# A fused convolution and expert-routing kernel: the second part's convolution moved into the first part's routing, one-hot matrices made apart, and a token load issued later

## The chip, the cores and the metric

The kernel runs on one core of one Trainium2 chip. The metric is the device time of the whole program in microseconds, the median of three executions. The profile is one further execution, taken by the hardware profiler; its span is 45 us shorter than the timed runs, so only differences are carried from one to the other.

## What is computed

The input `x` has 8 sequences of 3584 tokens of 192 channels. A causal convolution with 7 taps comes first: the taps are a softmax of `weight` over the 7 places, one set for each of 8 heads of 24 channels. Then each token goes through one of 8 experts:

```
logits     = y @ w_gate                      # 8 values a token
local_gate = sigmoid(y @ w_local)
e = argmax(logits)  if first of its sequence or local_gate < 0.5
    else the expert of the token before it
out = softmax(logits)[e] * relu(y @ w1[e]) @ w2[e]      # 192 -> 1024 -> 192
```

The expert of a token can depend on that of the token before, so routing is a scan along the sequence. Everything is in float32.

## The kernel before

**Parts and blocks.** The 28672 tokens are cut into 16 parts of 1792. Each part is convolved, its logits are taken, it is routed, and its rows (weight, token number, 192 channels) are scattered to a table in DRAM, `slots`, that has a region for each expert. In the text a *put* is one such scatter: `indirect_dma_start` of GpSimd, the line with `slots<-y_sb,posi`. A *block* is one unit of 128 rows of one expert (from block 35 on, mostly two units). For a block the kernel loads its rows back (`xg<-slots`, `load_rows`) and its expert's weights (`wb<-in_w`, `load_w`, 1.5 MB), transposes the rows on TensorE (`turn`), multiplies by the first matrix (`hidden`, hps), applies relu on ScalarE (hT), multiplies by the second (`output`, yps), adds the two halves on ScalarE (L961) and VectorE (L965) into `o_sb`, and scatters that to the output (`out_dram<-o_sb,xg`, L969). There are two buffers of `o_sb`, so the ScalarE step of block i waits until the output scatter of block i-2 has landed. Part 0 gives at least 7 full units, so blocks 0 to 6 need part 0 alone, and block 7 is the first that needs part 1 to be routed and all its puts landed.

**The first two parts** are done by another way than the later ones, because TensorE has nothing else to do: `wide` convolves by matmul (16 products with a banded matrix `hank`, 8 for each half of the part), turns the result (`turned`, 6 groups of transposes), takes the logits (`products`) and turns those back (`lps`, `lsb`, `ltp`, `lt`). `wide_route` then routes the part: VectorE finds the maximum and the local gate (`fc`), TensorE transposes it (`rps`), VectorE scans twice (`run`), TensorE transposes back (`bps`) and adds up the one-hot counts (`tot`, `within`), and VectorE makes the positions (`pos`, `posi`) and, for part 0, `first_table`, the list of the first seven units. Each of these is a Python generator that stops at its `yield`s; the calls of `next` decide how the two are woven together. All PSUM tiles called hps share four buffers, so a matmul into a fifth one waits for the eviction of an earlier one, and a tile that is still to be read (`rps`) takes one of the four out of the rotation meanwhile. In part 1 all evictions are ScalarE's.

**The first two blocks** are not read back from `slots`, because that would take too long. Their rows are picked from `ya` by one-hot matrices on TensorE: VectorE makes `hot` in 2 x 4 instructions (L526), and `gather` multiplies (L533, 16 products for each of the two blocks).

**Later parts** are convolved by multiply-add on VectorE (`conv`, L384, 48 instructions a part, the first tap by ScalarE, L374) and routed by `route`. Both are generators again, and `step(time)` runs about so many microseconds of them between the stages of a block. `x_in[g]` is the part's token load, 1920 KB (L115).

**Order of work.** The engines run the program's order: the kernel uses a manual schedule. All plain loads are in one queue, SyncE's, which the profile calls q1: weights, rows and tokens are issued in the program's order, and an issue that waits holds up those behind it. Indirect scatters are GpSimd's (q0). `load_w(j)` of block j is issued at block j-3, when the buffer of block j-4 is free; `load_rows` of block j waits for the puts of its part.

Of the kernel before, what the change touches and what calls it, by code (L numbers as in the profile page):

```python
# [8 lines left out]
F32 = mybir.dt.float32  # L9
I32 = mybir.dt.int32  # L10
Act = mybir.ActivationFunctionType
Alu = mybir.AluOpType
# [65 lines left out]
def kernel(  # L78
# [55 lines left out]
    with tc.tile_pool(name="scr", bufs=1) as scr:  # L134
        w = scr.tile([1, H, KC], F32, name="w")
        nc.scalar.dma_start(out=w, in_=weight.rearrange("(o h) k -> o h k", o=1))

        nc.sync.dma_start(out=hank, in_=wh)
        x_in = {0: load_b(0)}
        wg = cst.tile([P, 3 + DQ, Q], F32, name="wg")  # L140
        nc.scalar.dma_start(out=wg, in_=wgl)
        x_in[1] = load_b(1)
        nc.gpsimd.memset(ones, 1.0)
        any_ = scr.tile([1, 1], F32, name="any_")
        nc.scalar.activation(any_, ones[:1, :1], Act.Exp)
        make_identity(nc, ident)

        def awake(n):

            ps = hps_p.tile([P, 512], F32, name="hps")  # L150
            for _ in range(n):
                nc.tensor.matmul(ps[:, :P], lhsT=ones, rhs=ones, start=True, stop=True)

        awake(3)

        wide_w = scr.tile([P, 2 * H + H * KC], F32, name="wide_w")
        nc.vector.memset(wide_w, 0.0)
        wm = wide_w[:1, :H]
        nc.vector.tensor_reduce(wm, w, axis=AX.X, op=Alu.max)
        nc.vector.tensor_scalar(wm, wm, -1.0, None, Alu.mult)  # L160
        cps = hps_p.tile([P, 512], F32, name="hps")
        nc.tensor.matmul(cps[:, :H], lhsT=ones, rhs=wide_w[:, :H], start=True, stop=True)
        nc.vector.tensor_copy(nm, cps[:, :H])
        awake(7)
        ws = wide_w[:1, H:]
        wc = ws[:, H:].rearrange("o (h k) -> o h k", k=KC)
        nc.vector.tensor_tensor(w, w, bcast(wm, KC), op=Alu.add)
        nc.scalar.activation(w, w, Act.Exp)
        for h in range(H):
# [16 lines left out]
    def z_tile():  # L186
        return yt.tile([P, 3 * NH * TB + NB * DR], F32, name="z")

    def wide(g, xv, y_sb, zy, both):

        yT = zy[:, :3 * NH * TB].rearrange("p (u s) -> p u s", s=TB)
        yr = zy[:TB, 3 * NH * TB:].rearrange("p (b d) -> p b d", d=DR)
        lps = yps_p.tile([P, 512], F32, name="yps")[:, :4 * TB].rearrange("p (q s) -> p q s", s=TB)
# [64 lines left out]
        if both:  # L261
            nc.vector.tensor_copy(lsb[:, :2, :], lps[:, :2, :])
            nc.scalar.copy(lsb[:, 2:, :], lps[:, 2:, :])
        else:
            nc.scalar.copy(lsb, lps)
        ltp = yps_p.tile([P, 512], F32, name="yps")[:TB].rearrange("p (q c) -> p q c", c=P)
        for q in range(4):
            nc.tensor.transpose(ltp[:, q, :], lsb[:, q, :], identity=ident)
# [94 lines left out]
    def conv(g, x_sb):  # L363
        y_sb = row_tile()[:, :NT, :]
        got[g] = y_sb

        def cols(h):
            return y_sb[:, :, Y0 + h * GS:Y0 + (h + 1) * GS]

        def chans(h, k):  # L370
            return x_sb[:, k:k + NT, h * GS:(h + 1) * GS]

        def first(h):
            nc.scalar.activation(cols(h), chans(h, 0), Act.Copy, scale=c[:, h, 0:1])  # L374

        first(0)
        yield 0
        for h in range(H):
            if h + 1 < H:
                first(h + 1)  # L380
            if h == H // 2 and g + 1 < NPART:
                x_in[g + 1] = load_x(g + 1)
            for k in range(1, KC):
                nc.vector.scalar_tensor_tensor(cols(h), chans(h, k), c[:, h, k:k + 1],  # L384
                                               cols(h), Alu.mult, Alu.add)
                yield 0.6
# [3 lines left out]
    def wide_route(g, y_sb, lt):  # L390
# [29 lines left out]
        for a in range(2):  # L420
            nc.tensor.transpose(rps[:, a, :], fc[:, a, :], identity=tr)
        rs = sm.tile([P, NB], F32, name="rs")[:TB]
        nc.vector.tensor_reduce(rs, ex, axis=AX.X, op=Alu.add)
        nc.vector.tensor_scalar(rs, rs, 1e-9, None, Alu.add)
        nc.vector.reciprocal(rs, rs)
        yield
        run = sm.tile([NB, TB], F32, name="run")
        nf = sm.tile([NB, TB], F32, name="nf")
# [18 lines left out]
        tot = nps[:, :E * (1 + NB)].rearrange("p (e b) -> p e b", b=1 + NB)  # L447
        within = nps[:TB, E * (1 + NB):E * (1 + 2 * NB)]
        nc.tensor.matmul(tot[:, :, 0], lhsT=ones[:1, :], rhs=place[0:1, :], start=True, stop=True)
        yield  # L450
        oh = sm.tile([P, E, NB], F32, name="oh", bufs=1)[:TB]
        nc.vector.tensor_tensor(oh, bcast_mid(bps, E), bcast(en[:TB], NB), op=Alu.is_equal)
# [24 lines left out]
        yield  # L477
        if g == 0:
            first_table(upto[:, :, NB], pos)
        nc.vector.tensor_copy(place, upto[:, :, NB])  # L480
        nc.vector.tensor_tensor(base, place, eo, op=Alu.subtract)
        if g:
# [3 lines left out]
    def first_table(upto, pos):  # L486
# [33 lines left out]
        rel = sm.tile([P, 2, NB], F32, name="rel", bufs=1)[:TB]  # L520
        nc.vector.scalar_tensor_tensor(rel, bcast(r2[:TB], NB), -float(UT), bcast_mid(pos, 2),
                                       Alu.mult, Alu.add)
        for i in range(2):
            for b in range(0, NB, NB // 4):
                bs = slice(b, b + NB // 4)
                nc.vector.tensor_tensor(hot[:TB, i, bs, :], bcast(rel[:, i, bs], UT),  # L526
                                        bcast_mid(slot[:TB], NB // 4), op=Alu.is_equal)
        nc.vector.tensor_tensor(used, end[:, 1:], end[:, :E], op=Alu.subtract)

    def gather(i, y_sb, ps, blocks):  # L530

        for b in blocks:
            nc.tensor.matmul(ps[:, :Y0 + D], lhsT=hot[:TB, i, b, :], rhs=y_sb[:TB, b, :Y0 + D],  # L533
                             start=(b == 0), stop=(b == NB - 1))
# [440 lines left out]


    LEAD = 2
    st = {"conv": 1, "cgen": None, "route": 1, "rgen": None, "routed": 1}

    def start_conv():  # L980
        g = st["conv"] + 1

        free = not any(p[0] <= g - 3 for p in to_put)
        if st["cgen"] is None and g < NPART and g <= st["route"] + LEAD and free:
            st["conv"] = g
            st["cgen"] = conv(g, x_in.pop(g))
            next(st["cgen"])
# [20 lines left out]
    def step(time):  # L1008
# [17 lines left out]
    ya, yb = row_tile(), row_tile()  # L1026
    hot = row_tile().rearrange("p a b -> p (a b)")[:, :2 * NB * UT].rearrange(
        "p (i b s) -> p i b s", i=2, b=NB)
    for _ in wide(0, x_in.pop(0), ya, z_tile(), True):
        pass  # L1030
    x_in[2] = load_x(2)
    wide1 = wide(1, x_in.pop(1), yb, z_tile(), False)
    for i, _ in enumerate(wide_route(0, ya, got.pop(0))):
        for _ in range([4, 6, 0, 0, 0][i]):
            next(wide1)
    while to_put:
        put()
    for _ in wide1:
        pass

    wbs, xgs = {}, {}

# [21 lines left out]
    weights(AHEAD - 1)  # L1064


    picks = [yps_p.tile([P, 512], F32, name="yps") for _ in range(2)]
    more = wide_route(1, yb, got.pop(1))
    next(more)
    gather(0, ya, picks[0], range(NB // 2))  # L1070
    next(more)
    gather(0, ya, picks[0], range(NB // 2, NB))
    xgs[0] = gathered(picks[0])
    gather(1, ya, picks[1], range(NB // 2))
    next(more)
    step(2.4)
    xT, _ = turn(blocks[0][1], xgs[0])
    gather(1, ya, picks[1], range(NB // 2, NB))
    next(more)
    step(2.4)  # L1080
    xgs[1] = gathered(picks[1])
    for _ in more:
        pass
    for _ in range(6):
        put()
    for i, (_, n, _, _) in enumerate(blocks):
        ensure(i)
        weights(i + AHEAD)
        hT = hidden(n, wbs[i], xT)
        if i + 1 < len(blocks):  # L1090
            xT, copied = turn(blocks[i + 1][1], xgs[i + 1])
            if len(to_put) > NT // 2 and n == KT:
                put(copied)
        step(2.1 if n == 1 else 4.2)
        output(n, wbs.pop(i), xgs.pop(i), hT)
        step(1.3 if n == 1 else 3.0)
# [80 lines left out]
```

## Time and profile before

| | before |
|---|---|
| median of three executions | 1378.92 us (1378.63 to 1378.95) |
| span of the profiled execution | 1333.7 us |
| TensorE busy | 1315.8 us, 99% of the span |
| VectorE busy | 780.4 us, 59% |
| ScalarE busy | 512.1 us, 38% |
| GpSimd busy | 490.9 us, 37% |
| mean DMA rate | 255 GB/s |
| granted TensorE clock | 1.00 of full speed |

TensorE is nearly always busy, so what can change the time is where it waits. Its waits stand in the first 93 us: the convolution and routing of the first two parts until 49.7 us, and the first blocks after it. From there on a block of one unit follows the last every 5.5 us. A start time in an answer of the trace is counted from the start of the span; "x48" means 48 records of one kind, and what stands in brackets is the idle time of the engine before it and what ended that.

### The profile page before, as it was taken

How to read it: one execution, taken by the hardware profiler on the slowest of the kernel's cores; microseconds unless marked ns; L12 is line 12 of the kernel's file. 1: busy time of each engine (PE TensorE's matmuls, PEld its weight loads, DVE VectorE, ACT ScalarE, POOL GpSimd, SP SyncE). 2: the span in 40 equal slices, each digit the busy share in tenths (PEclk: the TensorE clock that was granted, in tenths of full speed). 3: DMA queues.
4: the chain of work that ended last, by engine and by line, in shares of the span. 5: the costliest groups of instructions: out<-in, count | busy, mean ns of one | idle time of the engine just before them, and what ended most of it. 6: DMA issues, size and time to landing. Idle time of an engine off the chain costs nothing. (4 is left out here: it accounts for less than half of the span.)

```text
span 1333.7 us, 41873 instructions
## 1 busy us (share of the span) xinstructions
PE 1315.8 (99%) x17140; PEld 1250.9 (94%) x17140; DVE 780.4 (59%) x2414; ACT 512.1 (38%) x1151; POOL 490.9 (37%) x534
## 2 busy tenths in 40 slices
PE   8989999999999999999999999999999999999998
PEld 7889999999999999999999999999999999999997
DVE  5989898877878787878787878786500000000000
ACT  5344444433333333333333333333333333333333
POOL 3734354434434343444343434343443211111111
PEclk9999999999999999999999999999999999999999
DMA  5899999976767576767676767565665555556893
GB/s 184 318 349 417 383 389 366 381 263 238 283 210 275 209 275 210 271 214 274 211 274 211 273 213 273 211 216 210 216 224 209 189 192 192 197 187 234 319 321 126
DMA packets 67299, 340.39 MB, mean 255 GB/s; under 512 B 12576, under 2 KB 23191, under 8 KB 47650
## 3 DMA queue, kind: packets, MB, share of 16 engines
q1 hardware_dynamic: 44640, 284.73, 58.9%
q0 software_dynamic: 22320, 52.82, 10.5%
q8 instruction: 136, 2.23, 0.7%
q14 instruction: 57, 0.47, 0.1%
q10 hardware_dynamic: 146, 0.15, 0.0%
HBM read 284.73 MB, written 53.41 MB: 254 GB/s over the span
## 5 line engine op out<-in xcount | busy, mean ns | idle before, releaser
L953 PE MATMUL yps<-wb,hT 64*128 64x192 f32 x7328 | 630.9, 325 | 3.9 <-ACT hT L942 3.4
L937 PE MATMUL hps<-xT,wb 64*128 64x256 f32 (+1 forms) x6816 | 627.0, 336 | 1.9 <-issue 1.9
L937 PEld LDWEIGHTS hps<-xT,wb 64*128 64x128 f32 x6816 | 560.3, 187 | 45.6 <-issue 2.9
L953 PEld LDWEIGHTS yps<-wb,hT 64*128 64x128 f32 x7328 | 597.1, 187 | 4.7 <-ACT hT L942 3.6
L969 POOL DMA_INDIRECT out_dram<-o_sb,xg x229 | 231.5, 1011 | 627.1 <-DVE o_sb L965 557.4
L384 DVE SCALAR_TENSOR_TENSOR y_sb<-x_sb,c,y_sb 128x336 f32<-128x336 f32 x672 | 383.6, 583 | 47.1 <-ACT y_sb L374 29.6
L942 ACT ACTIVATE hT<-hps 128x512 f32<-128x512 f32 (+1 forms) x568 | 261.1, 512 | 359.9 <-PE hps L937 359.8
L965 DVE SCALAR_TENSOR_TENSOR o_sb<-yps,xg,o_sb 128x192 f32<-128x192 f32 x229 | 87.4, 413 | 443.3 <-ACT o_sb L961 427.7
L754 POOL DMA_INDIRECT slots<-y_sb,posi x228 | 229.5, 1007 | 190.1 <-ACT hT L942 110.7
L961 ACT ACTIVATE o_sb<-yps,xg 128x192 f32<-128x192 f32 x229 | 86.8, 417 | 413.4 <-PE yps L953 404.5
L923 ACT COPY xT<-xps 128x768 f32<-128x768 f32 (+1 forms) x142 | 97.0, 683 | 1.9 <-PE xps L356 1.9
L356 PEld LDWEIGHTS xps<-ident,xg 64*128 64x128 f32 x1374 | 68.2, 139 | 8.4 <-DMA xg<-slots 0.3
L356 PE MATMUL xps<-ident,xg 64*128 64x64 f32 x1374 | 69.6, 222 | 0.1
L374 ACT ACTIVATE y_sb<-x_sb,c 128x336 f32<-128x336 f32 x112 | 63.6, 591 | 0.0
L549 DVE STREAM_TRANSPOSE z<-y_sb 128x768 f32<-128x768 f32 (+1 forms) x56 | 44.3, 846 | 0.1
L575 DVE COPY lt<-lq 32x36 f32<-32x36 f32 x224 | 41.7, 186 | 3.3
L559 PE MATMUL hps<-z,wg 64*32 64x128 f32 x1344 | 24.1, 273 | 0.4 <-issue 0.4
L559 PEld LDWEIGHTS hps<-z,wg 64*32 64x32 f32 x1344 | 19.5, 105 | 4.6 <-issue 3.1
L567 DVE STREAM_TRANSPOSE lq<-ls 128x256 f32<-128x256 f32 x14 | 6.2, 445 | 13.3 <-ACT ls L564 13.3
L545 POOL COPY y_sb<-y_sb 128x896 f32<-128x896 f32 x14 | 13.3, 948 | 0.1
L651 DVE COPY bk<-so_far 1x32 f32<-1x32 f32 x56 | 12.3, 219 | 0.7
L207 PE MATMUL hps<-x_sb,wb 118*112 118x192 f32 x64 | 11.7, 330 | 0.8 <-DMA x_sb<-in_xb_dram 0.8
(240 smaller groups left out, 370.8 us busy)
## 6 DMA issues: line engine op xcount, KB each, us to landing
wb<-in_w_dram SPq DMA_DIRECT2D x138, 1536.0 KB
x_sb<-in_x_dram SPq DMA_DIRECT2D x14, 1920.0 KB
xg<-slots SPq DMA_DIRECT2D x87, 259.0 KB
xg<-slots SPq DMA_DIRECT2D x53, 129.5 KB
wb<-in_w_dram SPq DMA_DIRECT2D x12, 512.0 KB
out_dram<-o_sb,xg POOLq DMA_INDIRECT x229
slots<-y_sb,posi POOLq DMA_INDIRECT x228
x_sb<-in_xb_dram SPq DMA_DIRECT2D x4, 768.0 KB
```

The costliest lines, as they stand in the source:

```text
L356: nc.tensor.transpose(to, src[rows], identity=ident[rows, rows])
L374: nc.scalar.activation(cols(h), chans(h, 0), Act.Copy, scale=c[:, h, 0:1])
L384: nc.vector.scalar_tensor_tensor(cols(h), chans(h, k), c[:, h, k:k + 1], cols(h), Alu.mult, Alu.add)
L549: nc.vector.transpose(z[:, t:u, :], y_sb[:, t:u, Y0:Y0 + D])
L754: ins = nc.gpsimd.indirect_dma_start(out=slots[:, :], in_=rows, in_offset=None, out_offset=bass.IndirectOffsetOnAxis(ap=to, axis=0)).ins
L923: copied = nc.scalar.copy(to, at)
L937: nc.tensor.matmul(hps[half][:, j, w], lhsT=wb[rows, f0:f0 + P], rhs=xT[rows, d, w], start=(d == 0 and j == 0), stop=(d == KD - 1), skip_g ...
L942: relu = nc.scalar.activation(hT[:, m:m + 2, w], hps[half][:, :, w], Act.Relu)
L953: nc.tensor.matmul(yps[half][:, k * D:(k + 1) * D], lhsT=hT[rows, m, k * P:(k + 1) * P], rhs=wb[rows, WA + m * D:WA + (m + 1) * D], start= ...
L961: nc.scalar.activation(o_sb[:, k, :], y[k][0], Act.Copy, scale=xg[:, k, 0:1])
L965: nc.vector.scalar_tensor_tensor(o_sb[:, k, :], y[k][1], xg[:, k, 0:1], o_sb[:, k, :], Alu.mult, Alu.add)
L969: sent = nc.gpsimd.indirect_dma_start(out=out, in_=o_sb[:, k, :], in_offset=None, out_offset=bass.IndirectOffsetOnAxis(ap=xg.bitcast(I32)[ ...
```

## The change

Four things are changed.

1. `wide` of part 1 starts earlier: two of its convolution products go between the logits of part 0 and the transposes that turn these back, and 7, 6 and 1 further steps go into the first three stages of part 0's routing, where 4 and 6 stood before. The 7 are products; the 6 are four products and the first two groups of transposes; the 1 is a product. The remaining steps follow part 0's routing. `wide` takes its own z tile.
2. The one-hot matrices are made by a function `hots(i)`: that of block 0 still in part 0's `first_table`, that of block 1 only after the first stage of part 1's routing. In part 1's routing the reciprocal of the softmax sum (`norm`) comes after the scans, not before. The gathers are cut at 4 and at 9 blocks of tokens, and the first four products of block 0's gather stand ahead of the transposes of part 1's logits.
3. The tokens of the fourth part, `x_in[3]`, are loaded at the start of block 3 and no longer in the middle of part 2's convolution; part 3's convolution may not start before block 6.
4. The gate weights `wg` are loaded on SyncE's queue, between the token loads of parts 0 and 1, and no longer on ScalarE's.

```diff
-        nc.scalar.dma_start(out=wg, in_=wgl)
+        nc.sync.dma_start(out=wg, in_=wgl)
...
-            if h == H // 2 and g + 1 < NPART:
+            if h == H // 2 and 2 < g < NPART - 1:
                 x_in[g + 1] = load_x(g + 1)
...
+        if g == 0:
+            norm()
         yield
...
         nc.tensor.matmul(tot[:, :, 0], lhsT=ones[:1, :], rhs=place[0:1, :], start=True, stop=True)
+        if g:
+            norm()
...
         if g == 0:
             first_table(upto[:, :, NB], pos)
+            hots(0)
...
+    LATE = 3
...
-        if st["cgen"] is None and g < NPART and g <= st["route"] + LEAD and free:
+        if (st["cgen"] is None and g < NPART and g <= st["route"] + LEAD and free
+                and (g != 3 or g in x_in and st["block"] > LATE + 2)):
...
-    for _ in wide(0, x_in.pop(0), ya, z_tile(), True):
-        pass
+    some(wide0, WIDE)
+    some(wide1, 2)
+    rest(wide0)
     x_in[2] = load_x(2)
-    wide1 = wide(1, x_in.pop(1), yb, z_tile(), False)
-    for i, _ in enumerate(wide_route(0, ya, got.pop(0))):
-        for _ in range([4, 6, 0, 0, 0][i]):
-            next(wide1)
+    route0 = wide_route(0, ya, got.pop(0))
+    for n in (7, 6, 1, 0, 0):
+        next(route0)
+        some(wide1, n)
...
-    next(more)
-    gather(0, ya, picks[0], range(NB // 2))
-    next(more)
-    gather(0, ya, picks[0], range(NB // 2, NB))
+    gather(0, ya, picks[0], range(4))
+    rest(wide1)
+    route1 = wide_route(1, yb, got.pop(1))
+    next(route1)
+    hots(1)
+    gather(0, ya, picks[0], range(4, NB))
+    next(route1)
     xgs[0] = gathered(picks[0])
-    gather(1, ya, picks[1], range(NB // 2))
-    next(more)
-    step(2.4)
+    picks.append(yps_p.tile([P, 512], F32, name="yps"))
+    gather(1, ya, picks[1], range(9))
+    next(route1)
+    step(1.8)
...
+        if i == LATE:
+            x_in[3] = load_x(3)
```

More of the change, by code (lines that the diff above doesn't have):

```diff
@@ L187, in z_tile, with wide @@
         return yt.tile([P, 3 * NH * TB + NB * DR], F32, name="z")
-    def wide(g, xv, y_sb, zy, both):
+    WIDE = 25
+    def wide(g, xv, y_sb, both):
+        zy = z_tile()
         yT = zy[:, :3 * NH * TB].rearrange("p (u s) -> p u s", s=TB)
@@ L265, in wide @@
             nc.scalar.copy(lsb, lps)
+        yield
         ltp = yps_p.tile([P, 512], F32, name="yps")[:TB].rearrange("p (q c) -> p q c", c=P)
@@ L422, in wide_route, with norm @@
         rs = sm.tile([P, NB], F32, name="rs")[:TB]
-        nc.vector.tensor_reduce(rs, ex, axis=AX.X, op=Alu.add)
-        nc.vector.tensor_scalar(rs, rs, 1e-9, None, Alu.add)
-        nc.vector.reciprocal(rs, rs)
+        def norm():
+            nc.vector.tensor_reduce(rs, ex, axis=AX.X, op=Alu.add)
+            nc.vector.tensor_scalar(rs, rs, 1e-9, None, Alu.add)
+            nc.vector.reciprocal(rs, rs)
+        if g == 0:
+            norm()
         yield
@@ L522, in first_table, with hots @@
                                        Alu.mult, Alu.add)
[L523 to L527, printed above, removed]
-        nc.vector.tensor_tensor(used, end[:, 1:], end[:, :E], op=Alu.subtract)
+        rels.append(rel)
+        nc.vector.tensor_tensor(used, end[:, 1:], end[:, :E], op=Alu.subtract)
+    rels = []
+    def hots(i):
+        for b in range(0, NB, NB // 4):
+            bs = slice(b, b + NB // 4)
+            nc.vector.tensor_tensor(hot[:TB, i, bs, :], bcast(rels[0][:, i, bs], UT),
+                                    bcast_mid(slot[:TB], NB // 4), op=Alu.is_equal)
     def gather(i, y_sb, ps, blocks):
@@ L977 @@
     LEAD = 2
-    st = {"conv": 1, "cgen": None, "route": 1, "rgen": None, "routed": 1}
+    LATE = 3
+    st = {"block": 0, "conv": 1, "cgen": None, "route": 1, "rgen": None, "routed": 1}
     def start_conv():
@@ L1028, with some, rest @@
         "p (i b s) -> p i b s", i=2, b=NB)
-    for _ in wide(0, x_in.pop(0), ya, z_tile(), True):
-        pass
+    wide0 = wide(0, x_in.pop(0), ya, True)
+    wide1 = wide(1, x_in.pop(1), yb, False)
+    def some(work, n):
+        for _ in range(n):
+            next(work)
+    def rest(work):
+        for _ in work:
+            pass
+    some(wide0, WIDE)
+    some(wide1, 2)
+    rest(wide0)
     x_in[2] = load_x(2)
-    wide1 = wide(1, x_in.pop(1), yb, z_tile(), False)
-    for i, _ in enumerate(wide_route(0, ya, got.pop(0))):
-        for _ in range([4, 6, 0, 0, 0][i]):
-            next(wide1)
+    route0 = wide_route(0, ya, got.pop(0))
+    for n in (7, 6, 1, 0, 0):
+        next(route0)
+        some(wide1, n)
     while to_put:
         put()
-    for _ in wide1:
-        pass
+    rest(route0)
+    some(wide1, WIDE - 16)
     wbs, xgs = {}, {}
@@ L1064 @@
     weights(AHEAD - 1)
-    picks = [yps_p.tile([P, 512], F32, name="yps") for _ in range(2)]
-    more = wide_route(1, yb, got.pop(1))
-    next(more)
-    gather(0, ya, picks[0], range(NB // 2))
-    next(more)
-    gather(0, ya, picks[0], range(NB // 2, NB))
+    picks = [yps_p.tile([P, 512], F32, name="yps")]
+    gather(0, ya, picks[0], range(4))
[5 more added lines that the diff above has]
+    next(route1)
     xgs[0] = gathered(picks[0])
-    gather(1, ya, picks[1], range(NB // 2))
-    next(more)
-    step(2.4)
+    picks.append(yps_p.tile([P, 512], F32, name="yps"))
+    gather(1, ya, picks[1], range(9))
+    next(route1)
+    step(1.8)
     xT, _ = turn(blocks[0][1], xgs[0])
-    gather(1, ya, picks[1], range(NB // 2, NB))
-    next(more)
+    gather(1, ya, picks[1], range(9, NB))
+    next(route1)
     step(2.4)
     xgs[1] = gathered(picks[1])
-    for _ in more:
-        pass
+    rest(route1)
     for _ in range(6):
@@ L1086 @@
     for i, (_, n, _, _) in enumerate(blocks):
+        st["block"] = i
         ensure(i)
         weights(i + AHEAD)
+        if i == LATE:
+            x_in[3] = load_x(3)
         hT = hidden(n, wbs[i], xT)
```

## The prediction

> **What bounds the kernel now.** I read the page's first part, then TensorE's waits, its timeline where they stand, and the queue behind each wait. TensorE is busy 1315.8 of 1333.7 us, so the change can only earn back single waits. After block 0 they are three. From the waits and TensorE's timeline:
>
> ```profile
> ACT o_sb L961 <- DMA out_dram<-o_sb,xg: 7.1, 1, 7.1
> PE yps L953 <- ACT hT L942: 3.4, 1, 3.4
> PEld xps L356 <- DMA xg<-slots: 0.3, 1, 0.3
> ...
> 23.15 0.35 PE L421 MATMUL hps<-ident,fc 112*16 112x112 f32 x2 [0.84 <-ACT y_sb L214]
> 40.19 0.36 PE L421 MATMUL hps<-ident,fc 112*16 112x112 f32 x2 [0.97 <-DVE fc L415]
> 49.73 2.95 PE L937 MATMUL hps<-xT,wb 64*128 64x128 f32 x48
> 59.20 2.70 PE L953 MATMUL yps<-wb,hT 64*128 64x192 f32 x29 [0.45 <-DVE o_sb L965]
> 73.91 2.87 PE L953 MATMUL yps<-wb,hT 64*128 64x192 f32 x32 [3.42 <-ACT hT L942]
> 92.35 0.40 PE L356 MATMUL xps<-ident,xg 64*128 64x64 f32 x6
> ```
>
> The first matmul of block 0 stands at 49.73. Block 1's output waits 0.45 us for VectorE's half of block 0's output. Block 3's output waits 3.42 us for ScalarE, which itself sat 7.1 us in L961 of block 2 because the output scatter of block 0 had not landed. The last line, the transposes of block 7's rows, waits 0.3 us for the rows: small, but it is the point at which part 1's puts and SyncE's queue meet TensorE. SyncE's queue and GpSimd's, and the busy time by stretch:
>
> ```profile
> 29.92 1.17 POOL L754 DMA_INDIRECT slots<-y_sb,posi  x1 [7.16 <-issue]
> 62.63 1.01 POOL L969 DMA_INDIRECT out_dram<-o_sb,xg  x1 [0.30 <-DVE y_sb L384]
> ...
> 53.33 1.49 SPq L890 DMA_DIRECT2D xg<-slots  x2
> 58.24 0.33 SPq L883 DMA_DIRECT2D wb<-in_w_dram  x1
> 58.63 0.45 SPq L115 DMA_DIRECT2D x_sb<-in_x_dram  x1
> 72.66 0.33 SPq L890 DMA_DIRECT2D xg<-slots  x1
> 73.56 3.62 SPq L883 DMA_DIRECT2D wb<-in_w_dram  x2
> 90.27 1.25 SPq L890 DMA_DIRECT2D xg<-slots  x2
> ...
> 50.00:58.00 8.00, 8.00 (x134) 8.00 (x134) 7.24 (x32) 3.24 (x9) 4.55 (x6) 1.00 0.54 137
> 58.00:74.00 16.00, 12.13 (x184) 11.70 (x180) 12.13 (x24) 5.39 (x15) 9.99 (x11) 1.00 1.03 409
> 74.00:92.00 18.00, 18.00 (x348) 17.58 (x348) 16.65 (x38) 8.21 (x24) 8.66 (x9) 1.00 0.84 327
> ```
>
> Sixteen puts of part 0 follow 29.92 at 1.245 us each (last at 49.24); then the rows of blocks 2 and 3 (53.33), then weights. From 58 us the 16 DMA engines are full (share 1.03, 409 GB/s) until about 88 us; the mean over 58 to 88 is 402 GB/s. The scatter issued at 62.63 lands only before 72.7. The rows of block 7 are issued at 90.27.
>
> **What the Trainium skill says.** "DMA: Bandwidth & Descriptors", section "Queues, rings and completion order": each DMA engine takes turns between the queues packet by packet, and within a ring consumes in order. The trace agrees: a scatter beside large weight and token packets took 9 us from the end of its issue. The same page, "Issuing engines are not separate DMA queues": all run on the same 16 engines, so moving `wg` to another queue adds no bandwidth; that load is not in any wait here. "Perfetto Trace Analysis", "Optimization Strategy": look for the gaps on the engine to be optimised and for the semaphore behind each; that gave the three above.
>
> **The change, part by part.**
>
> *Convolution of part 1 inside part 0's routing.* Nothing is added or removed; TensorE's order changes. Before, `rps` (L421) needed one ScalarE eviction and went at 23.15. Now nine convolution products precede it, and with four hps buffers it needs the sixth eviction. ScalarE is idle from 20.5 to 22.44 and can do two there; then the exponential (22.44, waits for VectorE) stands ahead of the rest, at 0.31 us each: the sixth ends at 24.0. `rps` goes at 24.1: +1.0. Between `rps` and `bps` now stand four products and eight transposes (8 x 0.10 us); the third product needs the eviction behind ScalarE's two copies L220 and L221 (0.52 us apart), and the transposes wait for the second scan because it frees the buffer of `rps`. That gives `bps` at 27.7 against 25.84 and the end of the totals at 29.1 against 27.1. So part 0's positions, its table and its puts come 2.0 us later: first put 31.9, last 51.2, rows of block 2 issued at about 55.3, and weights behind them equally late. What could hide it: nothing on GpSimd, whose puts are back to back.
>
> *One-hot matrices apart, `norm` later, gathers cut anew.* VectorE's work is the same. The four instructions of `hots(1)` (2.5 us, half of the 5.02 of L526) move behind part 1's `fc`. VectorE makes `hots(0)` from 34.6 to 37.1, `fc` by 39.75, `hots(1)` by 42.2, the second scan by 44.3. TensorE: first gathers 35.3 to 36.6, logits turned by 37.0, 12 gather products (24 records at 0.165) to 41.0, so the 0.97 wait before L421 is gone; nine more to 44.2, `bps` 44.4, transposes of block 0 to 45.1, seven more to 47.4, counts 47.6 (VectorE, after 0.7 for `norm` and four L384 at 0.58), block 0 at about 48.2: 1.5 us early.
>
> But VectorE does not follow. Its chain to the end of block 0's L965 holds the same instructions, starts 2.0 later and recovers the 1.4 us it sat idle at 42.84 waiting for ScalarE: L965 ends between 1 us earlier and 0.7 us later than 59.14, I take +0.3. Block 1's output would be ready at 58.2 - 1.5 and waits for that. So the 1.5 us are back in that wait, and TensorE runs on from about 59.5.
>
> *Tokens of part 3 in block 3.* Before, 1920 KB stood in the ring behind block 4's weights and ahead of block 5's rows and weights, and the scatter of block 0, issued at 62.63, shared the engines with them. Now block 5's rows (small) and weights stand there. The scatter is issued at 63.3, after the same eight puts, but more of these run beside the 512 KB chunks of block 3's weights, and the rows follow sooner. I expect it landed by 67 to 70.5, against 72.6; it is wanted at 66. So block 3's output starts at 70.8 to 71.7 instead of 73.91; the 3.42 us go wholly or largely. With them gone, block 7's transposes could start at 92.05 - 3.4 + 0.3 = 88.9.
>
> The load is not removed, however: it is now behind block 6's weights and ahead of block 7's, and block 7's rows stand behind all of them. The same bytes, 10.2 MB on SyncE's queue and about 2.1 MB of scatters at 402 GB/s, 31 us, lie ahead of these rows as before, and the stream begins 2.0 us later. Before, block 7's weights were moved by 87.3 with stragglers to 89, and then the queue was empty until part 1's last put had landed and the rows went at 90.27. Now the puts land earlier (about 86) and the rows are already queued: 89 + 2.0, less 0.3 for one put more done before the stream starts, plus 0.4 for 129.5 KB: about 91.0. TensorE waits there 2 us, and block 7 starts 1.3 us earlier than at 92.35. What is behind that wait: the whole rest of TensorE's order.
>
> *Part 3's convolution from block 6.* VectorE idles some 6 us about 85 to 91. It is at 59% and has nothing to do in the last quarter of the span; part 3 is needed from block 35. Its first ScalarE instruction waits for the tokens, which land about 86, before it is reached at 90. Cost nothing. `wg` lands some us later, is needed at 14.78: nothing.
>
> **The rivals.**
>
> 1. *Likeliest: the wait moves to block 7's rows.* For it: DMA share 1.03 in the stretch, the ring's order. Gain 1.3 us: 1377.6.
> 2. *Faster: the rows come in time.* The queue was empty from 89 to 90.3, so bandwidth was not the last limit before, and the rate may be above 402 when small packets are spread otherwise. Then the gain is that of the removed wait, 92.35 - 88.9 = 3.4: 1375.5. Against it: block 7's weights and 1920 KB stand ahead.
> 3. *Slower: the 2.0 us of part 0's routing show.* Every put, row and weight of the first blocks hangs on them; if the stream also keeps its stragglers and the engines lose some throughput to the turns, block 7 starts at 94.4 to 96, or a ScalarE wait for tokens or for scatters of blocks 1 to 4 comes back beside the late token load: +2 to +3.7, about 1382.0. Against it: before, 4 us passed between the end of the stream and block 7, and half of these are now used.
>
> **How the numbers follow.** I give 0.50, 0.31 and 0.19. The bound of 0.2% is 2.76 us. Case 1 gives 0.04 faster, 0.45 same and 0.01 slower; case 2 0.27 faster and 0.04 same; case 3 0.03 same and 0.16 slower. The forecast is 1377.6. The range takes in case 2 to its middle (1375.2) and case 3 up to +2.1 (1381.0); the unknown is one scatter's landing (67 to 70.5) and the stream's end (plus or minus 1.5 us).
>
> **What would show it.** First put at 31.9 and `rps` at 24.1; block 0 at 48.2; a longer wait of block 1's output for L965 (0.45 to about 3 us); no wait, or under 1 us, at block 3's output; rows of block 7 issued about 87 with a wait of about 2 us at their transposes, at 91. Wrong if block 7's transposes start below 89.5 (rival 2) or above 94 (rival 3), or if a new wait appears after 93 us.

## The result, and the profile after

| | us, median | range | ratio to before, 95% interval |
|---|---|---|---|
| before | 1378.78 (6 runs) | 1376.51 to 1379.57 | |
| after | 1368.10 (6 runs) | 1365.55 to 1369.86 | 0.9923 (0.9910 to 0.9936) |

The change makes the kernel 0.8% faster. The forecast was 1377.6 (1375.2 to 1381.0): the time lies below the range.

The profiled execution of before took 1335.45 us, its timed ones 1379. The profiled execution of after took 1369.86, as its timed ones did. So the two pages are not a pair, and what lies between them had to be found first. TensorE's waits after, with the total, the number and the longest in us:

```profile
PE hps L453 <- DVE run L451: 6.3, 1, 6.3
PE yps L969 <- ACT hT L958: 4.5, 16, 0.3
PE hps L953 <- issue: 4.1, 8, 0.9
```

None of the three waits of before is there. In their place stand one long wait for VectorE ahead of block 0, sixteen short ones for the relu, and stops in which TensorE waits for nothing that the profile shows ("issue"). The timeline after, for TensorE, VectorE and GpSimd:

```profile
41.21 0.36 PE L425 MATMUL hps<-ident,fc 112*16 112x112 f32 x2 [1.57 <-DVE ex L412]
...
48.10 1.05 PE L549 MATMUL yps<-y_sb 112*128 112x194 f32 x3 [0.39 <-issue]
55.41 0.27 PE L453 MATMUL hps<-ident,run 16*112 16x16 f32 x1 [6.26 <-DVE run L451]
...
62.22 3.15 PE L953 MATMUL hps<-xT,wb 64*128 64x128 f32 x48
...
70.64 0.51 PE L953 MATMUL hps<-xT,wb 64*128 64x128 f32 x4 [0.45 <-issue]
72.10 0.47 PE L953 MATMUL hps<-xT,wb 64*128 64x128 f32 x3 [0.95 <-issue]
...
53.19 0.26 DVE L438 COPY nf<-hps 16x112 f32<-16x112 f32 x1 [9.62 <-remote]
...
49.70 0.94 POOL L770 DMA_INDIRECT slots<-y_sb,posi  x1 [0.30 <-issue]
64.90 0.94 POOL L770 DMA_INDIRECT slots<-y_sb,posi  x1 [14.26 <-ACT hT L958]
```

TensorE's transposes in L425 are over at 41.6. VectorE's copy of them (L438) starts at 53.19: the signal (the semaphore change that lets VectorE go on) is 11 us late, and VectorE sits idle for 9.62 of them. GpSimd issues part 0's sixteen puts back to back from 30.06 on, the last from 49.70 to 50.64. In block 1 (68 to 76) TensorE gets through one to four products each 0.7 to 1.5 us, while GpSimd issues part 1's first puts back to back from 64.90 to 74.8. The granted clock falls in these stretches (the length and TensorE's busy time stand behind the window, the granted clock third from the end):

```profile
0.00:42.00 42.00, 36.98 (x240) 29.80 (x241) 23.10 (x87) 20.94 (x52) 18.11 (x65) 1.00 0.60 214
42.00:80.00 38.00, 25.96 (x190) 23.10 (x192) 20.42 (x65) 6.77 (x21) 16.63 (x17) 0.69 0.55 190
80.00:110.00 30.00, 29.03 (x498) 27.24 (x497) 21.83 (x42) 11.69 (x33) 13.24 (x13) 1.00 0.86 316
```

The Trainium skill, "TensorE: Matmul & The Clock Gate", Part 1, says that TensorE's clock is halved after an idle window of about 3.4 us and released after a busy one. The trace agrees in the length: the stretches at half clock last 3.4, 6.8 and 13.7 us. It does not agree that the window has to be idle: in the 3.41 us ahead of each of the three TensorE was busy for 1.50, 1.78 and 1.42 us. The first begins at 42.2, behind the wait of 1.57 us; in block 1 the stop begins at 68 and the half clock at 72.9. So the half clock follows the stops and does not start them.

### The profile page after: what moved, and what is told of

Same layout as the page of the kernel before. It is cut to its first block, busy times and chain, and to the rows that moved or that the text cites. A ratio compares the mean times of both kernels' runs of the same rounds, so it can differ in the third digit from the quotient of the medians.

```text
span 1368.2 us, 41873 instructions
## 1 busy us (share of the span) xinstructions
PE 1335.7 (98%) x17140; PEld 1299.4 (95%) x17140; DVE 776.1 (57%) x2414; ACT 513.8 (38%) x1151; POOL 490.8 (36%) x534
## 3 DMA queue, kind: packets, MB, share of 16 engines
q0 software_dynamic: 22320, 52.82, 10.2%
## 5 line engine op out<-in xcount | busy, mean ns | idle before, releaser
L969 PE MATMUL yps<-wb,hT 64*128 64x192 f32 x7328 | 650.9, 326 | 7.8 <-ACT hT L958 4.5
L953 PE MATMUL hps<-xT,wb 64*128 64x256 f32 (+1 forms) x6816 | 640.6, 337 | 4.3 <-issue 4.1
L969 PEld LDWEIGHTS yps<-wb,hT 64*128 64x128 f32 x7328 | 607.1, 187 | 18.8 <-ACT hT L958 10.2
L953 PEld LDWEIGHTS hps<-xT,wb 64*128 64x128 f32 x6816 | 608.2, 188 | 15.3 <-issue 7.3
L388 DVE SCALAR_TENSOR_TENSOR y_sb<-x_sb,c,y_sb 128x336 f32<-128x336 f32 x672 | 377.1, 571 | 19.4 <-issue 1.4
L360 PEld LDWEIGHTS xps<-ident,xg 64*128 64x128 f32 x1374 | 79.8, 139 | 3.5
L360 PE MATMUL xps<-ident,xg 64*128 64x64 f32 x1374 | 79.6, 222 | 0.0
L549 PE MATMUL yps<-y_sb 112*128 112x194 f32 x64 | 16.2, 411 | 2.2 <-issue 1.7
L549 PEld LDWEIGHTS yps<-y_sb 112*128 112x128 f32 x64 | 14.2, 244 | 3.4 <-issue 3.3
```

The source lines that it names most:

```text
L360: nc.tensor.transpose(to, src[rows], identity=ident[rows, rows])
L953: nc.tensor.matmul(hps[half][:, j, w], lhsT=wb[rows, f0:f0 + P], rhs=xT[rows, d, w], start=(d == 0 and j == 0), stop=(d == KD - 1), skip_g ...
L969: nc.tensor.matmul(yps[half][:, k * D:(k + 1) * D], lhsT=hT[rows, m, k * P:(k + 1) * P], rhs=wb[rows, WA + m * D:WA + (m + 1) * D], start= ...
```

## The experiments

In each batch the kernel before ran beside the others. It took 1377 to 1380 us in three batches and 1334 to 1336 in three. I name the first "with late signals" and the second "without"; the reason for the name follows from the first batch. The expectations of the first batch weigh two theories: A, the time lies in TensorE's clock; B, it lies in the waits and queues of the first blocks.

**First batch, with late signals (before 1377.98): the kernels again, and the two halves of the change.** Late only is before with this edit; weave only is after without it:

```diff
-            if h == H // 2 and g + 1 < NPART:
+            if h == H // 2 and 2 < g < NPART - 1:
                 x_in[g + 1] = load_x(g + 1)
...
+                and (g != 3 or g in x_in and st["block"] > LATE + 2)):
...
+        if i == LATE:
+            x_in[3] = load_x(3)
```

> The kernel before, unchanged, profiled again beside the others. Theory A (the clock): its timed runs of about 1378.8 us are not like the profiled run of 1335.5 us; a run of 1378 us shows a granted clock well under 0.999 over the span, about 0.984 or less, with the slow matmuls inside the first 100 us, and by 110 us it stands later than the kernel after does. Theory B (waits and queues): the clock is as in the kernel after (0.990 to 0.991) or better, and the 10.6 us are found in waits of TensorE (3.4 us at block 3's output, some more at block 7's rows).

> The kernel after, unchanged: 1365.6 to 1369.9 us, clock 0.990 to 0.991. Theory A: its slow stretches are again at about 42 to 80 us and fewer than those of the kernel before on the same chip. Theory B: clock the same for both; the ratio is made by waits.

> Only the tokens of the fourth part move to block 3 and its convolution to blocks after the fifth; the order of TensorE before block 0 is that of the kernel before. Theory A: the stretch in which TensorE's clock is cut lies before or at block 0, which this edit does not touch, so the time is within 3 us of the kernel before, 1375 to 1380. Theory B (queues): nearly the whole gain is here, 1367 to 1371.

> The kernel after with the tokens of the fourth part loaded as in the kernel before (block 2's convolution of part 2 loads them), so only the order of the convolution, the one-hot matrices, the gathers and the queue of wg differ from before. Theory A: nearly the whole gain is here, 1366 to 1371, clock about 0.99. Theory B: 1375 to 1382, since the wait for block 0's scatter and its tokens is still there.

| | us | ratio | interval |
|---|---|---|---|
| before again | 1378.92 | 1.0003 | 0.9992 to 1.0013 |
| after again | 1366.14 | 0.9918 | 0.9901 to 0.9936 |
| late only | 1364.58 | 0.9909 | 0.9894 to 0.9924 |
| weave only | 1379.91 | 1.0012 | 1.0004 to 1.0021 |

Theory A falls: before and after have the same clock (0.992 and 0.991), and the weave brings nothing. The whole gain is in the later tokens. But theory B falls too, since the gain is not in the first blocks. From the starts of ScalarE's relus, in us ("to block 2" is from the span's start to block 2's first relu):

```text
                    to block 2   blocks 2-40   40-100   100-end
before, profiled          63.3         252.1    666.8     351.6
before again              83.0         263.8    677.0     352.1
after again               82.0         261.1    667.0     352.2
weave only                81.2         263.1    677.0     352.1
late only                 84.3         260.4    666.0     352.1
```

Of 13.7 us between the traces of before again and after again 10.0 lie in blocks 40 to 100, where neither the tokens of part 3 nor any row is waited for. (The first trace of after takes 671.3 us there, so the size varies from run to run; the other 3.7 us were not traced to a cause.) There the blocks of two units (256 rows) take 10.80 us each, except where the logits of a part (L559, 48 products) stand between them. Before, part 7's logits and what surrounds them (TensorE, then GpSimd, then ScalarE):

```profile
421.96 1.59 PE L559 MATMUL hps<-z,wg 64*32 64x128 f32 x96
423.48 6.04 PE L937 MATMUL hps<-xT,wb 64*128 64x256 f32 x48
...
434.99 5.34 PE L937 MATMUL hps<-xT,wb 64*128 64x256 f32 x47
...
423.28 0.99 POOL L969 DMA_INDIRECT out_dram<-o_sb,xg  x1 [3.40 <-DVE o_sb L965]
424.57 0.99 POOL L969 DMA_INDIRECT out_dram<-o_sb,xg  x1 [0.30 <-issue]
...
426.18 0.43 ACT L564 COPY ls<-hps 128x128 f32<-128x128 f32 x2 [3.57 <-remote]
```

After, on the same occasion:

```profile
418.12 5.37 PE L953 MATMUL hps<-xT,wb 64*128 64x256 f32 x48
423.30 0.56 PE L360 MATMUL xps<-ident,xg 64*128 64x64 f32 x12
423.78 1.59 PE L575 MATMUL hps<-z,wg 64*32 64x128 f32 x96
425.31 5.47 PE L969 MATMUL yps<-wb,hT 64*128 64x192 f32 x64
430.61 5.35 PE L953 MATMUL hps<-xT,wb 64*128 64x256 f32 x48
...
425.23 1.02 POOL L770 DMA_INDIRECT slots<-y_sb,posi  x1 [1.87 <-DMA wb<-in_w_dram]
...
426.64 0.43 ACT L580 COPY ls<-hps 128x128 f32<-128x128 f32 x2 [0.99 <-PE hps L575]
```

The same 48 products stand in another place. Before, they follow the output and precede the hidden layer; after, they follow the transposes and precede the output. That is so for all ten parts from 6 to 15, because the convolution of part 3, started later, shifts every later part's routing by about half a block. Before, the products are over at 423.55, but ScalarE's copies start at 426.18, 0.62 us after the second of the block's two output scatters (424.57 + 0.99). The logits hold two of the four `hps` buffers until then, so the second half of the hidden layer waits: 6.04 us in place of 5.34. After, one put is in the way, the copies are 1.27 us late, and what follows is the output, which needs no `hps`.

This gave theory C (the place on TensorE) and theory D: a signal of TensorE that falls due while GpSimd is in an indirect DMA arrives only when that, or the run of them, is over. The trace also records when a semaphore changes, and these records show that it is the signal that is late, not its reader: in before again the two signals of part 7's logits stand at 426.16 and 426.20, 2.6 us after the records of their last products end, and the first copy starts 0.02 us later. In the first trace of after, four signals of products that ended at 39.64 to 49.15, L425's among them, stand together at 53.12 to 53.37.

ScalarE has 737 instructions for a hidden layer, an output or logits that wait for a signal of TensorE. Late by over 0.5 us, counted from the end of the last product's record, are:

```text
                  due in an indirect DMA   due otherwise   late ones that start 0.2-0.8 us
                        late / all           late / all    after the end of an indirect DMA
before, profiled          1 / 317              0 / 420            0
before again             41 / 360              6 / 377           43
after again              35 / 370              1 / 367           33
```

The six others of before again fall due within 0.4 us of the end of an indirect DMA.

**Second batch, with late signals (before 1377.15): the place, and the scatters.** Hoist is before with the logits of parts 6 to 15 held for the place of after; lower is after with the logits behind the output, as on TensorE in before (3 in place of 1):

```diff
         yield "hop"
+        while g >= 6 and st["at"] != 1:
+            yield "hop"
...
+        st["at"] = 1
         step(2.1 if n == 1 else 4.2)
+        st["at"] = 2
         output(n, wbs.pop(i), xgs.pop(i), hT)
+        st["at"] = 3
         step(1.3 if n == 1 else 3.0)
+        st["at"] = 0
```

Scatter is before with nothing moved (2 in place of 1, which leaves the order on TensorE, ScalarE and VectorE) and one more wait on GpSimd; puts is after with another place for the puts:

```diff
+            if st["ls"] is not None:
+                tc.add_manual_dep(sent.ins, st["ls"].ins.name, SYNC, reason="logits first")
...
-            put(relu)
+            if two:
+                put(relu)
+                put(relu)
```

> The kernel before, in which the local-gate and router logits of parts 6 to 15 (48 products, L559) are held until the step between a block's transposes and its output, as they lie in the kernel after; tokens of part 3 are loaded as before. Theory C (order of the logits on TensorE): it recovers most of the gain, 1367 to 1373 us; the block with logits takes 23.3 us in place of 23.9 and the next block 21.6 in place of up to 22.5. Theory B (the later load and its waits in the first eight blocks): 1376 to 1380.

> The kernel after, in which the logits of parts 6 to 15 are held until the step behind a block's output, as they lie in the kernel before; everything else as after. Theory C: most of the gain is lost, 1373 to 1378. Theory B: 1364 to 1368, as the kernel after.

> The kernel before with TensorE's, ScalarE's and VectorE's order unchanged; in a block that is followed by logits (parts 6 to 15), the two output scatters on GpSimd wait until ScalarE has copied the logits. Theory D (a signal of TensorE that falls into an indirect DMA of GpSimd arrives only when that is over): the copies come within 0.3 us of the last product in place of 2.6, the block takes about 23.4, and the time is 1368 to 1374. If it is the order on TensorE alone (C without D): the copies stay late, 1376 to 1381.

> The kernel after, in which both puts of a block stand behind the last relu of its hidden layer (before, one behind the first pair's relu and one behind the last). Theory D: in blocks of 64 tokens the last signal of the hidden layer no longer falls into a put; the pace goes from 6.1 to about 5.5 us for a half block wherever it was 6.1, some 10 to 14 us in all: 1352 to 1358. Otherwise (the lateness is not tied to the puts): 1364 to 1370.

(The 23.3, 23.4, 23.9 and 21.6 us in these texts are of two blocks. A half block is a block of one unit, a whole block one of two; a unit has 128 rows, and the "64 tokens" in these texts should be one unit.)

| | us | ratio | interval | blocks 2-40 | 40-100 |
|---|---|---|---|---|---|
| hoist | 1367.72 | 0.9930 | 0.9911 to 0.9950 | 262.0 | 669.1 |
| lower | 1378.64 | 1.0009 | 1.0000 to 1.0019 | 260.0 | 685.0 |
| scatter | 1365.19 | 0.9915 | 0.9896 to 0.9934 | 262.0 | 666.1 |
| puts | 1376.86 | 1.0001 | 0.9988 to 1.0015 | 255.2 | 688.1 |

The place carries the change: with it before gains what after has, and without it after has nothing. Lower loses more than that in blocks 40 to 100, 18 us against after again where before again loses 10, because there the products themselves take 2.1 to 4.1 us beside the two scatters; its first 40 blocks are shorter. Hoist came as theory C expected; lower lies just above the range. And scatter shows why the place counts. Its products stand where before has them; only the two scatters wait:

```profile
419.86 1.59 PE L560 MATMUL hps<-z,wg 64*32 64x128 f32 x96
421.39 5.45 PE L938 MATMUL hps<-xT,wb 64*128 64x256 f32 x48
...
421.49 0.43 ACT L565 COPY ls<-hps 128x128 f32<-128x128 f32 x2 [0.81 <-PE hps L560]
...
422.20 0.99 POOL L970 DMA_INDIRECT out_dram<-o_sb,xg  x1 [4.38 <-ACT ls L565]
423.50 0.99 POOL L970 DMA_INDIRECT out_dram<-o_sb,xg  x1 [0.30 <-issue]
```

The copies come 0.04 us after the last product (2.63 before), the hidden layer takes 5.45 us, and the kernel reaches the time of after with a wait added, faster than the 1368 to 1374 expected. The signals of the logits stand at most 0.03 us after the products' ends in all ten parts. C without D falls; D stands.

Puts was expected at 1352 to 1358 and missed. Its first half is as expected. Before, in half blocks, a put stood at the end of the hidden layer, the last relus came 1.4 us late, and the output's second half waited:

```profile
272.12 1.57 PE L953 MATMUL yps<-wb,hT 64*128 64x192 f32 x16 [0.29 <-ACT hT L942]
...
271.68 0.66 ACT L942 ACTIVATE hT<-hps 128x256 f32<-128x256 f32 x2 [1.98 <-PE xps L356]
...
270.15 0.97 POOL L754 DMA_INDIRECT slots<-y_sb,posi  x1 [0.30 <-issue]
```

With both puts behind the last relu a half block takes 5.5 us in place of 6.1, and blocks 2 to 40 take 5.9 us less than in after again and 8.6 less than in before again. But in whole blocks the two puts, now together, meet the logits' products in their new place: these take 3.4 to 4.2 us in place of 1.6, and blocks 40 to 100 cost 11 us more than in before again. The edit was too wide. That the same mechanism slows the products is likely, but not shown apart.

**Third to fifth batch, without late signals (before 1334.32, 1335.54 and 1334.78).** Half is puts with the puts left apart in whole blocks. Hold adds to half the held scatters, with the logits back behind the output as in scatter. Split and spread are after with other places for the puts of parts 0 and 1:

```diff
-            put(relu)
+            if n > 1:
+                put(relu)
+            elif two:
+                put(relu)
+                put(relu)
...
-    while to_put:
-        put()
+    for _ in range(8):
+        put()
     rest(route0)
...
+    while to_put:
+        put(st["nf"])
     step(1.8)
...
-    for _ in range(6):
-        put()
```

The first hunk is half, the next two are split (`st["nf"]` is VectorE's copy L438), the last is spread. All is half, split and hold together.

> The kernel after, in which both puts of a block stand behind the last relu in blocks of 64 tokens only (i.e. half blocks); in whole blocks they stay apart. Theory D: the half blocks keep the pace of 5.5 us (8 to 10 us gained by block 18), and the logits of parts 6 to 15 meet one put at most as in the kernel after: 1355 to 1360. Without D: 1364 to 1370.

> As the last, and besides the logits of parts 6 to 15 behind the output, with the two scatters of that block held until ScalarE has copied the logits. Theory D: the place of the logits on TensorE is of no weight once no indirect DMA runs beside them: 1354 to 1360, within 2 us of the last. If the place on TensorE costs by itself (C): 1365 to 1370.

> The kernel after, in which 8 of part 0's 16 puts stand behind VectorE's first copy of part 1's transposed flags (L438) in place of ahead of it. Theory D: TensorE's signal for this copy comes 0.5 us after the eighth put, at about 41 to 43 us in place of 51.6, and block 0 starts at 55 to 58 in place of 60.7: 1360 to 1365. If the wait is the clock's or TensorE's own: the copy stays at about 50 and the puts end later, 1366 to 1372.

> The kernel after without the six puts of part 1 that stand back to back ahead of block 0; they go one behind each relu like the others. Theory D: TensorE's stop in block 1 (about 8 us, 67 to 75) shrinks to under 2 us; against it stands that part 1's rows are complete later, by some 5 us, which block 7 may wait for: 1358 to 1364. Without D: no change or slower by the later rows, 1366 to 1374.

> The kernel after, unchanged. Where signals are late (before at 1377 to 1379): 0.992 of before again. Where they are not (before at 1334): the prediction's own case, 1331.5 to 1334, 0.998 to 1.000 of before, since the logits' place then costs 0.2 us for each part at most.

> The kernel after with both puts behind the last relu in half blocks. Where signals are late, theory D: 1355 to 1360. Where they are not: 1331.9 as seen.

> The last, with part 0's puts split (8 of 16 behind VectorE's copy of part 1's flags, L438) and the logits of parts 6 to 15 behind the output with that block's scatters held. Where signals are late, theory D: L438 runs at 41 to 43 us in place of 51.6 and the time is 1348 to 1356, the fastest of all. Where they are not: 1330 to 1333.

> The kernel after with the three edits of the run before (puts behind the last relu in half blocks, part 0's puts split, scatters held behind the logits). Where signals are late (before at 1377 to 1379), theory D: L438 at 41 to 43 us in place of 51.6, half blocks at 5.5 us in place of 6.1, logits copied within 0.3 us of the last product; 1348 to 1356. If lateness is not tied to indirect DMAs: 1364 to 1370. Where they are not late (before at 1334): 1330 to 1332 as seen.

| | us | ratio | interval |
|---|---|---|---|
| half | 1331.88, again 1332.44 | 0.9981, 0.9982 | 0.9973 to 0.9989, 0.9970 to 0.9994 |
| hold | 1331.50 | 0.9974 | 0.9961 to 0.9987 |
| split | 1333.75 | 0.9991 | 0.9981 to 1.0001 |
| spread | 1349.38 | 1.0111 | 1.0092 to 1.0129 |
| after | 1332.79 | 0.9984 | 0.9974 to 0.9994 |
| all | 1331.01, again 1331.61 | 0.9979, 0.9977 | 0.9965 to 0.9993, 0.9968 to 0.9986 |

These batches fell where the kernel before takes 1334 us, so the numbers expected for half, hold, split and spread with late signals could not be tested there. Their traces, like that of before in the first place, have next to no late signal (none to two each by the count above). So one and the same kernel has two times, 3% apart, and the profile before showed one of them while the table showed the other. After, half (again) and all lie within what was expected of them without late signals, to 0.5 us. Spread is slower than before: TensorE waits 5.8 us for VectorE and 2.9 us for a relu between 90 and 105 us, with the clock halved behind these waits, and ends 15 us later. The six puts ahead of block 0 are needed there.

After, without late signals, is the case that the prediction worked out:

```profile
46.95 1.82 PE L953 MATMUL hps<-xT,wb 64*128 64x128 f32 x26
...
71.09 2.87 PE L969 MATMUL yps<-wb,hT 64*128 64x192 f32 x32 [1.33 <-ACT hT L958]
...
91.43 0.40 PE L360 MATMUL xps<-ident,xg 64*128 64x64 f32 x6 [1.93 <-DMA xg<-slots]
91.67 4.50 PE L969 MATMUL yps<-wb,hT 64*128 64x192 f32 x32
...
87.82 1.28 SPq L906 DMA_DIRECT2D xg<-slots  x2
```

**Last batch, with late signals (before 1380.29).**

> As the run before it. Where signals are late (before at 1377 to 1379), theory D: L438 at 41 to 43 us, half blocks at 5.5 us, 1348 to 1356. Where they are not (before at 1334): 1330 to 1332.

> The kernel before with the tokens of part 3 loaded in block 3 and its convolution from block 6, nothing else. Where signals are late: 1364 to 1366, as seen. Where they are not (before at 1334): the wait of block 3's output for the scatter (3.4 us) goes, a wait for block 7's rows of up to 2 us comes; if the prologue gives nothing, as predicted, the time is that of the kernel after, 0.998 to 0.999 of before; if the prologue gives the gain, 0.9995 to 1.001.

| | us | ratio | interval | to block 2 | blocks 2-40 | 40-100 |
|---|---|---|---|---|---|---|
| all | 1354.91 | 0.9819 | 0.9801 to 0.9836 | 76.4 | 258.4 | 666.9 |
| late only | 1365.84 | 0.9893 | 0.9877 to 0.9910 | 82.2 | 261.5 | 668.8 |

All met its expectation of 1348 to 1356 us. Its trace has 17 late signals by the count above, that of late only 42. It is faster than before on both kinds of occasion, by 1.8% where signals are late; by its median it is faster than after too, though with late signals the two were not timed in one batch. Its prologue, VectorE, GpSimd, then TensorE:

```profile
43.10 0.26 DVE L438 COPY nf<-hps 16x112 f32<-16x112 f32 x1
...
40.53 0.94 POOL L771 DMA_INDIRECT slots<-y_sb,posi  x1 [0.30 <-issue]
43.63 0.94 POOL L771 DMA_INDIRECT slots<-y_sb,posi  x1 [2.17 <-DVE nf L438]
...
49.20 1.83 PE L954 MATMUL hps<-xT,wb 64*128 64x128 f32 x26
53.16 0.90 PE L954 MATMUL hps<-xT,wb 64*128 64x128 f32 x10 [2.13 <-PE hps L954]
...
69.28 2.87 PE L954 MATMUL hps<-xT,wb 64*128 64x128 f32 x47
```

With a gap of 2.17 us after the eighth put, L438 runs at 43.10 in place of 51.6 to 53.2, with no wait at all, and block 0 starts at 49.20, earlier than the 55 to 58 expected of the split. But the other eight puts and six of part 1 then run beside block 0, which takes until 69.28. So a good part of the stop moved rather than went; by block 2 the kernel is 6.6 us ahead of before again and 5.8 ahead of late only. The late-only run again has the gain of after; that part of its expectation which asked for the other kind of occasion stays untried.

## Why the prediction was wrong

The step that failed is «Part 3's convolution from block 6 … Cost nothing.» I asked whether VectorE had time for the part and when its tokens land, and did not follow what the delay does to the parts behind it. In each of the ten parts from 6 to 15 it moves the 48 products of the logits from behind an output to ahead of it. That is 10.0 of the 13.7 us between the traces with late signals. Hoist and lower show that the place carries it, and scatter that it counts because of the two output scatters beside the products. A new wait after 93 us, which the prediction named as a sign of being wrong, shows in after too, in most of TensorE's sixteen short waits for a relu; but before again has seventeen, so they belong to the occasion and not to the change.

It could be mispriced because of an earlier step: «TensorE is busy 1315.8 of 1333.7 us, so the change can only earn back single waits. After block 0 they are three.» That is true of the profiled execution. The timed ones took 45 us more, and I carried differences from one to the other as if the 45 us were spread evenly. They are not: of the 42.2 us between the two traces of before 19.7 lie ahead of block 2, 11.7 in blocks 2 to 40 and 10.2 in blocks 40 to 100, where signals are late and TensorE stops. Without late signals two blocks with logits between them take 23.46 us in before and 23.44 in after; with late signals the place costs about 1 us for a part (10.0 for ten).

Point by point, against the trace of after without late signals. First product is at 7.18 there and at 8.27 in the profile before; it is at 6.94 in the other trace of before, so this moves by itself. Differences to before are counted from it, so that 1.1 us are added to the times of after; the times themselves are printed as the trace has them.

- *Convolution inside part 0's routing:* `rps` +1.0, `bps` +1.9, first put +2.0 us; predicted +1.0, +1.9 and +2.0. Right.
- *Block 0* starts 1.7 us earlier, predicted 1.5. Right. *Block 1's output* waits 0.71 us for VectorE, predicted about 3; in its place the hidden layer of block 0 waits 1.2 us for VectorE. Right in kind; the two waits together are shorter than the 3 us.
- *Block 3's output:* predicted no wait or under 1 us, at 70.8 to 71.7; measured 71.09, or 72.2 counted from the first product, with 1.33 left of the 3.42. The size was somewhat off.
- *Block 7's rows:* a wait of 1.93 us, predicted 2. Right in kind. But the rows are issued at 87.82 and the transposes start at 91.43, and counted from the first product that is 88.9 (predicted 87) and 92.5 (predicted 91.0): no earlier than the 92.35 of before. The 1.3 us that the forecast rests on are not there. What I did not see is what the wait does: the clock is halved for 3.4 us behind it, and block 6's output takes 4.50 us in place of 2.8.
- *The sum:* the paired runs there give 0.9984 (0.9974 to 0.9994), some 2 us; predicted 1.3. That this is near is luck, for it does not come from block 7. At block 8 the kernel is 0.8 us behind the profile before, 1.8 counted from the first product; it gains 1.1 us between blocks 14 and 16 and 0.8 between 34 and 36, both where the logits of an early part have changed their place.

Rival 2 (faster, rows in time) was on the right side for a reason that is not its own: with late signals TensorE waits for no rows in either kernel, and without them those of block 7 are waited for. Weave only, at 1.0012 with late signals, shows that the 2.0 us of the prologue cost next to nothing there, against rival 3.

Open is why signals are late on some occasions and not on others, and why of those due in an indirect DMA only about a tenth were. Two things on record bear on it. The chip alone does not decide: by the record's numbers signals were late on chips 2, 0 and 11 and not on 7, 0 and 13, so chip 0 had both. And traces with late signals hold 11396 to 12597 records of semaphore changes, those without 16669 to 16879; the recording itself differs, and whether it takes part in holding the signals up is untested. With so many records missing, a wait that such a trace puts down to "issue" may have had a releaser.

## What to carry to other kernels

Set the span of the profile against the timed runs before reading it: a gap of 3% says that the waits in the timed runs are not those on the page. When an edit delays one stage of a pipeline that repeats, list what it moves in every later round on every engine, and look at what the moved work stands beside on the others. Work on TensorE whose result frees a buffer that the very next work needs is best not placed where GpSimd issues indirect DMAs, if signals can be late as here: hold these, or put the work ahead of something that does not need the buffer.

## What the runs showed of the hardware

- On some occasions a signal of TensorE that falls due while GpSimd is in an indirect DMA (0.94 to 1.35 us each) can arrive only 0.4 to 0.6 us after its end: 1.3 us late for one, 2.6 for two in a row. Beside the run of sixteen puts the signal that VectorE's copy L438 waits for was 6 to 12 us late; it came up to 2.8 us after the last put (late only again), but in three traces already behind the twelfth or thirteenth, and not at a fixed 0.4 to 0.6 us. On other occasions at most two of ScalarE's 737 waits in a trace are over 0.5 us late, with the same kernel: 1334 against 1378 us.
- On the occasions with late signals TensorE itself slows to one to four products each 0.7 to 1.5 us beside a run of puts, without any wait in the trace; in lower and puts, two indirect DMAs beside the logits' products were enough (up to 4.2 us in place of 1.6).
- Such stops are followed by half the clock on TensorE for 3.4 to 13.7 us. The window ahead need not be idle: in the trace of after without late signals a wait of 1.93 us was enough, with TensorE busy for 1.48 of the 3.41 us ahead.
